# A windowed attention and MLP kernel: head-halves order in the first batch, additive masks through TensorE, strided reads when transposed tiles leave PSUM, full-depth sink values, score units in pairs

## The chip, the core and the metric

The kernel runs on one NeuronCore of a Trainium2 chip. TensorE (PE) multiplies matrices into PSUM, VectorE (DVE) and ScalarE (ACT) read PSUM and work on SBUF, GpSimd (POOL) works on SBUF alone, and SyncE (SP) issues every DMA from one queue, in program order. Each engine runs its own instructions in order; semaphores tie the engines together. The metric is device microseconds for one launch.

## The reference

Four batches, eight heads, 768 positions, head size 64. Attention with 4 sink positions and a window of 128, then a residual MLP over the 512 features, with a product over tokens in front:

```python
scores = q @ k.T / 8                       # per head, 768 x 768
keep = (col < 4) | ((row - col >= 0) & (row - col < 128))
a = softmax(where(keep, scores, -1e9))
x = (a @ v) as [batch, 768, 512]
a1 = alpha1 * x + beta1
u  = x + lam * einsum('ts,bsd->btd', w_tok, a1)
a2 = alpha2 * u + beta2
out = u + lam * (relu(a2 @ w_ch1) @ w_ch2) # 512 -> 2048 -> 512
```

All inputs and outputs are float32 in DRAM; the kernel works in fp16 with fp32 sums.

## The kernel before

**Tiles.** The sequence is six tiles of 128 rows. Heads come in four pairs (`hp`), and G is a half of the heads (four of them, two pairs). A window of 128 means that key tile j meets query tiles j and j+1 only, so a score unit (j, G) is 128 keys by 256 queries by four heads.

**Attention of a batch.** `load_qk` brings q or k of a head pair (eight DMAs of 384 KB, six buffers), `cast_qk` makes it fp16, and `trans` does six TensorE transposes into one PSUM tile `tp` and copies that to `qkT` on VectorE (L175). Partition p of a loaded tile holds six neighbouring positions, so the copy has to interleave: before, it reads PSUM in order and writes every sixth fp16 element of SBUF. `sinks` multiplies all queries from 256 on with the four sink keys and takes the exponential (`es`). `scores` does four matmuls (L200, each on 64 rows of the array), one exponential over 128x1024 (L207) into `E`, and `mask` multiplies `E` with a 0/1 mask on VectorE (L218). `pv` multiplies `es` with the sink values `vs` (L227, 64 rows) and two `E` tiles with `vf`, which has a column of ones for the sum of the softmax; `norm` divides (L250, L251) and, with both halves there, makes `xh` on GpSimd (L257, L258). `vs` is filled by eight small DMAs out of `vf`.

**Dense part of a batch.** `dense` gives a list of slots: six `tok` (six matmuls of 512 columns, an add L310, an fp16 cast L312), `uT` (transposes of that, L325, and a scale and shift on VectorE, L330), 32 `mlp1` (four matmuls of 384 columns, L345, and a Relu on ScalarE, L350), and 24 `mlp2` (four of 512 columns, L362; after four slots an add, L368, and the store). Transposes, `tok`, `uT`, `mlp1`, `mlp2` and the sinks share three PSUM buffers (tag "d").

**What sets the order.** The schedule is written out by hand. The first batch's attention is in line, mixed with loading and casting the weights; then a loop over batches walks the slots of `dense(b)` and after slot i runs `side[i]`: the next batch's casts, transposes, sinks, score units and `pv`, spread evenly over the slots, and for b = 0 the casting and loading of the MLP weights. Weights pass through two staging buffers (tag "wst"), so a weight's DMA waits on SP for the cast of the weight two before it, and everything behind it on SP waits too.

Of the kernel before, what the change touches and what calls it, by code (L numbers as in the profile page):

```python
# [14 lines left out]
def kernel(  # L15
# [20 lines left out]
    P = 128  # L36
# [12 lines left out]
    assert window == P and 0 < n_sink <= 16, (n_sink, window)  # L49
# [11 lines left out]
    def load_qk(b, hp, t):  # L61
        nat = sb.tile([P, 2, NR * D], FP32, tag="nat", bufs=6, name=f"nat{b}_{hp}_{t}")
# [43 lines left out]
    )  # L106

# [38 lines left out]
    def cast_qk(b, hp, t, eng):  # L146
        nat = nat_tiles.pop((b, hp, t))
        d = sb.tile([P, NR, P], FP16, tag="n16", bufs=4, name=f"n16_{b}_{hp}_{t}")
        o = d.rearrange("p r (e d) -> p e r d", e=2)
        i = nat.rearrange("p e (r d) -> p e r d", r=NR)  # L150
# [27 lines left out]
    def sinks(b):  # L178
        for e in range(2):
            nc.vector.tensor_copy(  # L180
                ks[64 * e : 64 * e + 64, :, e * n_sink : (e + 1) * n_sink],
                qkT[b].rearrange("p (a t) s -> p a t s", t=2)[64 * e : 64 * e + 64, :, 1, 0:n_sink],
            )
        pt = ps.tile([P, S - 2 * P], FP32, tag="d", bufs=3, name=f"sk{b}")
        for hp in range(HP):
# [58 lines left out]
    def norm(b, r, G):  # L244
        po = pv_ps.pop((b, r, G))
        if G == 0:
            x_t[b, r] = sb.tile([P, H, D], FP32, tag="x", bufs=12, name=f"x{b}_{r}")
        x = x_t[b, r]
# [4 lines left out]
        if G == 1:  # L253
# [325 lines left out]
```

## Time and profile before

| | |
|---|---|
| median of 3 runs | 383.55 us (382.33 to 385.0) |
| profiled execution: time, span | 382.78 us, 381.1 us |
| PE, DVE, ACT, POOL busy | 286.6, 206.8, 132.5, 120.9 us |
| first score matmul starts | 31.24 us |
| `tok` of batch 0, 1, 2, 3 starts | 70.90, 165.85, 245.30, 326.13 us |
| first `mlp1` of batch 0, first `mlp2` of batch 0 | 80.23, 135.97 us |
| mean granted TensorE clock | 0.928 of full speed |

The span runs from the first to the last instruction. Since the matmuls of `tok` open each batch's dense part, their starts cut the span into periods: 0 to 165.85 us holds the first batch's attention and dense part with the second batch's attention, then come two alike periods, and from 326.13 us the last dense part alone. The sum of busy times says little by itself, because these stretches have different limits.

### The profile page before, as it was taken

Reading aid. Unit: us, or ns where it says so; the run is one execution under the profiler, and the core shown is the slowest. Engines: PE = TensorE matmul, PEld = TensorE weight load, DVE = VectorE, ACT = ScalarE, POOL = GpSimd, SP = SyncE. Lnnn points to the kernel's source line nnn. Section 1 sums busy time; section 2 is a strip of 40 time slices with the busy share of each in tenths; the row PEclk is TensorE's granted clock in tenths of the full one; section 3 lists DMA queues with packets and bytes.
Section 4 is the critical chain, followed back from the end, with each engine's and each line's share of the span. In section 5 each row is a group of like instructions: output and inputs, shape, how many; then the busy total and the mean of one; then the engine's idle time right before and its main releaser. Section 6 shows DMA issues by size and latency. Waiting matters only on the chain.

```text
span 381.1 us, 4896 instructions
## 1 busy us (share of the span) xinstructions
PE 286.6 (75%) x1956; PEld 144.9 (38%) x1956; DVE 206.8 (54%) x289; ACT 132.5 (35%) x208; POOL 120.9 (32%) x121
## 2 busy tenths in 40 slices
PE   1313655899336699996649999984489999999996
PEld 1211422355113244443425544443245444455542
DVE  6894576255299566539983434279924443440021
ACT  1004536186101363212229731022258520267300
POOL 3200298308276035674001452723004425000000
PEclk9999965699955699999899999999989999999999
DMA  7912662339960009542000039340000011100012
GB/s 248 328 30 83 140 221 98 124 105 344 264 212 15 2 22 306 141 140 55 0 2 0 3 120 269 138 138 0 0 2 0 3 55 57 55 3 0 10 74 83
DMA packets 43927, 37.03 MB, mean 97 GB/s; under 512 B 27393, under 2 KB 35585, under 8 KB 43905
## 3 DMA queue, kind: packets, MB, share of 16 engines
q1 hardware_dynamic: 43904, 36.73, 31.2%
q8 instruction: 15, 0.25, 0.3%
q14 instruction: 8, 0.06, 0.0%
HBM read 30.41 MB, written 6.29 MB: 96 GB/s over the span
## 4 chain that ended last, share of the span: by engine, by line
PE 56%; DVE 26%; DMA 5%; ACT 3%; SPq 3%; issue 3%; POOL 3%; DVEq 0%; ACTq 0%
PE ch L362 22%; DVE qkT L175 19%; PE h L345 16%; PE tok L305 7%; PE S L200 3%; PE pv L235 2%; DMA wst_w<-in_moe_w_ch_dram 2%; PE pv L227 2%; DMA vnat<-in_v_dram 2%; PE tp L174 1%; PE pv L239 1%; ACT w1f L429 1%; SPq L166 1%; DMA la_b<-in_moe_alpha_dram 1%; DVE w2f L435 1%
## 5 line engine op out<-in xcount | busy, mean ns | idle before, releaser
L345 PE MATMUL h<-uT,w1f 128*128 128x384 f16 x512 | 101.0, 344 | 12.8 <-DVE qkT L175 11.8
L362 PE MATMUL ch<-w2f,hT 128*128 128x512 f16 x384 | 89.9, 379 | 0.0
L175 DVE COPY qkT<-tp 128x768 f16<-128x768 f16 x32 | 84.5, 2774 | 7.7 <-PE tp L174 7.6
L350 ACT ACTIVATE hT<-h 128x384 f16<-128x384 f32 x128 | 61.9, 492 | 74.3 <-PE h L345 73.6
L345 PEld LDWEIGHTS <-w1f 128*128 128x128 f16 x512 | 48.7, 101 | 49.1 <-issue 24.9
L257 POOL TENSOR_TENSOR tmp<-x,la_b 128x512 f32<-128x512 f32 x24 | 30.9, 1287 | 109.6 <-DVE x L251 109.6
L207 ACT ACTIVATE E<-S 128x1024 f16<-128x1024 f32 x40 | 40.9, 1022 | 36.4 <-PE S L200 36.3
L174 PE MATMUL tp<-iden,n 128*128 128x128 f16 x192 | 19.5, 256 | 42.4 <-DVE n L154 18.9
L368 DVE TENSOR_TENSOR x<-x,ch 128x512 f32<-128x512 f32 x24 | 16.5, 688 | 63.9 <-PE ch L362 63.9
L362 PEld LDWEIGHTS <-hT 128*128 128x128 f16 x384 | 34.7, 98 | 38.8 <-issue 2.7
L218 DVE TENSOR_TENSOR E<-E,maskn 128x1024 f16<-128x1024 f16 x32 | 27.4, 857 | 26.9 <-ACT E L207 26.8
L312 ACT CAST u<-x 128x512 f16<-128x512 f32 x24 | 14.8, 617 | 71.3 <-DVE x L310 69.0
L305 PE MATMUL tok<-xh,wtokT 128*128 128x512 f16 x144 | 35.3, 401 | 2.2 <-POOL xh L258 1.3
L258 POOL TENSOR_TENSOR xh<-tmp,lb_b 128x512 f16<-128x512 f32 x24 | 34.5, 1437 | 1.9
L174 PEld LDWEIGHTS <-n 128*128 128x128 f16 x192 | 15.8, 116 | 50.0 <-DVE n L154 19.7
L154 POOL CAST n<-nat 128x768 f16<-128x768 f32 x28 | 23.5, 845 | 32.4 <-issue 24.1
L310 DVE TENSOR_TENSOR x<-x,tok 128x512 f32<-128x512 f32 x24 | 16.5, 687 | 16.7 <-PE tok L305 16.6
L305 PEld LDWEIGHTS <-wtokT 128*128 128x128 f16 x144 | 14.5, 102 | 20.9 <-issue 5.7
L251 DVE TENSOR_TENSOR x<-pv,rec 128x256 f32<-128x256 f32 x48 | 20.4, 424 | 1.8 <-DVE rec L250 0.2
L435 POOL TENSOR_TENSOR w2f<-wst_w,lam_b 128x512 f16<-128x512 f32 x8 | 13.5, 1704 | 20.5 <-DMA wst_w<-in_moe_w_ch_dram 20.5
L162 POOL CAST vf<-vnat 128x512 f16<-128x512 f32 x24 | 16.2, 675 | 10.7 <-DMA vnat<-in_v_dram 6.9
L235 PE MATMUL pv<-vf,E 128*128 128x65 f16 x160 | 17.1, 205 | 2.3 <-DVE x L251 2.3
(47 smaller groups left out, 183.0 us busy)
## 6 DMA issues: line engine op xcount, KB each, us to landing
wst_w<-in_moe_w_ch_dram SPq DMA_DIRECT2D x8, 1024.0 KB
nat<-in_q_dram SPq DMA_DIRECT2D x16, 384.0 KB
nat<-in_k_dram SPq DMA_DIRECT2D x16, 384.0 KB
vnat<-in_v_dram SPq DMA_DIRECT2D x24, 256.0 KB
out_dram<-x SPq DMA_DIRECT2D x24, 256.0 KB
wst_t<-in_moe_w_tok_dram SPq DMA_DIRECT2D x3, 768.0 KB
vs<-vf SPq DMA_DIRECT2D x32, 0.5 KB
lam_b<-in_moe_lam_dram SPq DMA_DIRECT2D x1, 256.0 KB
```

What stands on the lines that cost most here:

```text
L154: eng.tensor_copy(o, i)
L174: nc.tensor.transpose(pt[:, r, :], src[:, r, :], iden)
L175: nc.vector.tensor_copy(qkT[b][:, 2 * hp + t, :].rearrange("p (i r) -> p r i", r=NR), pt)
L207: nc.scalar.activation(eT, pS, AF.Exp, scale=scale)
L218: nc.vector.tensor_mul(ev, ev, m.to_broadcast(list(ev.shape)))
L235: nc.tensor.matmul(po[:, hl, :], E[b, r - 1, G][:, e, i, P : 2 * P], vf[r - 1][:, h, :], start=(r == 1), stop=False,)
L257: nc.gpsimd.tensor_mul(tmp, xf, la1_b)
L258: nc.gpsimd.tensor_add(xh, tmp, lb1_b)
L305: nc.tensor.matmul(pt, wtokT[:, si, ti * P : (ti + 1) * P], xh_t[b, si], start=(si == 0), stop=(si == NR - 1),)
L345: nc.tensor.matmul(ph, w1f[:, c, fi * P : (fi + 1) * P], uT[0][:, c, chk * NTOK : (chk + 1) * NTOK], start=(c == 0), stop=(c == NC - 1),)
L350: nc.scalar.activation(hT[chk][:, fi, :], ph, AF.Relu)
L362: nc.tensor.matmul(pch[ti], hT[chk][:, fi, nt * P : (nt + 1) * P], w2f[:, fi, :], start=(fi == 0), stop=(fi == NF - 1),)
```

## The change

1. **Strided read.** `trans` writes the transposes to PSUM as before; the copy to `qkT` now reads PSUM with a step of 128 fp16 elements (256 bytes) and writes SBUF in order. In the first batch two of the eight copies are on ScalarE.
2. **First batch by head halves.** Two head pairs are loaded, cast and transposed; their six score and six `pv` steps run while the other two pairs are cast and transposed; then the other half follows. Masks are not multiplied: two matmuls per unit with the identity put -30000 or 0 into PSUM, and the score matmuls add to it. `xh` leaves out beta1, which comes back in `residual` as the row sum of `w_tok` times lam times beta1.
3. **Loads.** All of the first batch, the sink values, the constants, `w_tok` and the first quarter of `w_ch1` are issued at the start into buffers that stand idle then. The later weight loads stay behind the two staging buffers. The prefetch has eight q/k tiles in place of six.
4. **Casts of weights.** `w_tok` is cast in six pieces: three in the second half of the attention, three between the `tok` slots of batch 0. Each quarter of `w_ch1` is cast half on ScalarE, half on GpSimd. Batch 0 walks `mlp1` by quarters of `w_ch1`.
5. **Later batches.** The sink product is 128 rows deep (`vs` is zero where a head has no business) and `vs` is filled by one GpSimd multiply from a DMA of its own. Two score units stand back to back. Every third Relu is on VectorE.

```diff
-        pt = ps.tile([P, NR, P], FP16, tag="d", bufs=3, name=f"tp{b}_{hp}_{t}")
+        pt = ps.tile([P, S], FP16, tag="d", bufs=3, name=f"tp{b}_{hp}_{t}")
+        o = qkT[b][:, 2 * hp + t, :]
         for r in range(NR):
-            nc.tensor.transpose(pt[:, r, :], src[:, r, :], iden)
-        nc.vector.tensor_copy(
-            qkT[b][:, 2 * hp + t, :].rearrange("p (i r) -> p r i", r=NR), pt)
+            nc.tensor.transpose(pt[:, r * P : (r + 1) * P], src[:, r, :], iden)
+        copy(eng or nc.vector, o.rearrange("p (i r) -> p i r", r=NR),
+             pt.rearrange("p (r i) -> p i r", r=NR))
...
+        if bias:
+            bt = bias0 if j == 0 else (biasn if j < NR - 1 else biasn[:, :, 0:P])
+            for e in range(2):
+                nc.tensor.matmul(pS[:, e], iden, bt.to_broadcast([P, n, w]), start=True, stop=False)
...
-            g = slice(64 * G, 64 * G + 64)
+            g = slice(64 * G, 64 * G + 64) if b == 0 else slice(0, P)
...
+    def fill_vs(b):
+        nc.gpsimd.tensor_mul(vs[b % 2][:, :, 0:D], vsn.pop(b), bmf.to_broadcast([P, H, D]))
...
-        def mk_s(i):
+        def mk_s(j):
             def f():
-                sc[i] = scores(b, *S_ORDER[i])
+                if j < NR - 1:
+                    for G in range(2):
+                        sc[j, G] = scores(b, j, G)
...
-                nc.scalar.activation(hT[chk][:, fi, :], ph, AF.Relu)
+                if fi % 3 == 2:
+                    nc.vector.tensor_scalar_max(hT[chk][:, fi, :], ph, 0.0)
+                else:
+                    nc.scalar.activation(hT[chk][:, fi, :], ph, AF.Relu)
...
+    def cast_wtok(ti, eng):
+        w = sb.tile([P, NR, P], FP16, tag="n16", bufs=4, name=f"wt16_{ti}")
+        wf = w.rearrange("p r i -> p (r i)")
+        nc.scalar.activation(wf, wtn[ti // 3][:, ti % 3, :], AF.Copy, accum_out=rs[:, ti : ti + 1])
+        pt = ps.tile([P, NR, P], FP16, tag="d", bufs=3, name=f"wT{ti}")
+        for si in range(NR):
+            nc.tensor.transpose(pt[:, si, :], w[:, si, :], iden)
+        copy(eng, wtokT[:, :, ti * P : (ti + 1) * P], pt)
...
+    for (hp, t), ce, ee in zip(QK_ORDER[:4], (V, A, G_, V), (V, A, V, A)):
+        cast_qk(0, hp, t, ce)
+        trans(0, hp, t, ee)
...
+    scores(0, 0, 0, True)
+    scores(0, 1, 0, True)
+    sinks(0, (0,))
...
+    scores(0, 4, 1, True)
+    cast_wtok(1, V)
+    cast_v0(1, 5, G_)
+    pvn0(3, 1)
+    scores(0, 5, 1, True)
+    cast_wtok(2, V)
+    pvn0(4, 1)
+    pvn0(5, 1)
     load_w1(1)
...
+    tok[0]()
+    cast_wtok(3, V)
+    tok[1]()
+    cast_wtok(4, V)
+    tok[2]()
+    cast_wtok(5, V)
+    for f in uT0:
+        f()
+    tok[3]()
+    tok[4]()
+    tok[5]()
+    cast_w1(1, (A, G_))
     load_w1(3)
...
-            side[6].append(lambda: (cast_w1(2), load_w2(0)))
-            side[10].append(lambda: (cast_w1(3), load_w2(1)))
-            side[20].append(lambda: (cast_w2(0), load_w2(2)))
-            side[24].append(lambda: (cast_w2(1), load_w2(3)))
-            side[28].append(lambda: cast_w2(2))
-            side[32].append(lambda: cast_w2(3))
+            side[5].append(lambda: (cast_w1(2, (A, G_)), load_w2(0)))
+            side[12].append(lambda: (cast_w1(3, (A, G_)), load_w2(1)))
+            side[19].append(lambda: (cast_w2(0, (V, G_, V, G_)), load_w2(2)))
+            side[23].append(lambda: (cast_w2(1, (V, G_, V, G_)), load_w2(3)))
+            side[27].append(lambda: cast_w2(2, (V, G_, V, G_)))
+            side[31].append(lambda: cast_w2(3, (V, G_, V, G_)))
...
             if b == 0:
-                side[11].append(lambda nb=nb: prefetch(nb))
+                side[6].append(lambda nb=nb: prefetch(nb))
```

**Order on ScalarE where the dense part of batch 0 begins.** `wt16` is a sixth of `w_tok` in fp16, `u16` the cast after a `tok`, `w1f` the cast of a quarter of `w_ch1`. Before:

```order
L429 CAST w1f_118<-wst_w1_0_308 128x4x512
L207 ACTIVATE E0_5_None_529<-S0_5_None_520 128x1024
L429 CAST w1f_118<-wst_w1_1_350 128x4x512
L312 CAST u16_0_0_591<-x0_0_301 128x512
L312 CAST u16_0_1_601<-x0_1_370 128x512
L312 CAST u16_0_2_611<-x0_2_417 128x512
```

The same place in the changed kernel:

```order
L472 ACTIVATE wt16_2_543,rs_71<-wtn0_109 128x768
L208 CAST w1f_165<-wst_w1_0_113 128x2x512
L391 CAST u16_0_0_597<-x0_0_244 128x512
L472 ACTIVATE wt16_3_599,rs_71<-wtn1_115 128x768
L391 CAST u16_0_1_618<-x0_1_270 128x512
L472 ACTIVATE wt16_4_620,rs_71<-wtn1_115 128x768
L391 CAST u16_0_2_639<-x0_2_306 128x512
L472 ACTIVATE wt16_5_641,rs_71<-wtn1_115 128x768
```

Three casts of `w_tok` now stand behind the `u16` of the `tok` before them; on PE their transposes stand between the `tok` matmuls, as the diff shows.

**Order of the DMAs on SP around the first prefetch.** `w2` are quarters of `w_ch2`, `nat1` and `vnat1` q, k and v of batch 1. Before:

```order
L387 DMA wst_w2_0_653<-in_moe_w_ch2_dram 128x4x512
L387 DMA wst_w2_1_685<-in_moe_w_ch2_dram 128x4x512
L64 DMA nat1_0_0_693<-in_q_dram 128x2x384
L64 DMA nat1_0_1_695<-in_k_dram 128x2x384
L64 DMA nat1_1_0_697<-in_q_dram 128x2x384
```

Now:

```order
L69 DMA vnat1_2_793<-in_v_dram 128x8x64
L69 DMA vnat1_3_795<-in_v_dram 128x8x64
L77 DMA vsn1_797<-in_v_dram 32x8x64 x4
L110 DMA wst_w2_1_840<-in_moe_w_ch2_dram 128x4x512
L110 DMA wst_w2_2_888<-in_moe_w_ch2_dram 128x4x512
L110 DMA wst_w2_3_943<-in_moe_w_ch2_dram 128x4x512
```

Before, two quarters of `w_ch2` went ahead of the prefetch and two behind it; now one goes ahead (row not shown) and three follow the whole prefetch.

**Order on VectorE behind the second quarter of `w_ch2`**, in the changed kernel:

```order
L487 TENSOR_TENSOR w2f_166<-wst_w2_1_840,lam_b_66 128x512 x2
L210 COPY qkT1_908<-tp1_1_0_947 128x768
L210 COPY qkT1_908<-tp1_1_1_966 128x768
L210 COPY qkT1_908<-tp1_2_0_985 128x768
L430 TENSOR_SCALAR hT0_0_707<-h0_0_14_994 128x384
L210 COPY qkT1_908<-tp1_2_1_1002 128x768
L487 TENSOR_TENSOR w2f_166<-wst_w2_2_888,lam_b_66 128x512 x2
L210 COPY qkT1_908<-tp1_3_0_1021 128x768
L210 COPY qkT1_908<-tp1_3_1_1036 128x768
```

Six of the eight copies of batch 1 stand behind this multiply. Before, seven stood behind the third quarter's multiply (L435) and three behind the fourth's; now two stand behind the third's and none behind the fourth's.

## Rows read from the trace of the kernel before

**Rows 1.** Chain that ended last, in time: start us, us, what.

```profile
192.86 5.28 DVE qkT L175 x2
...
338.98 17.70 PE h L345 x108
356.68 20.73 PE ch L362 x96
```

**Rows 2.** Busy by stage: stretch, length, PE, PEld, DVE, ACT, POOL, clock, DMA share, GB/s.

```profile
171.10:198.97 27.87, 15.92 (x125) 9.45 (x124) 25.85 (x21) 6.26 (x13) 4.95 (x7) 0.94 0.09 20
198.97:245.30 46.33, 45.82 (x333) 21.65 (x334) 17.82 (x40) 21.35 (x35) 20.51 (x19) 1.00 0.34 103
...
250.55:278.17 27.62, 14.58 (x125) 8.82 (x124) 25.84 (x21) 6.25 (x13) 4.94 (x7) 1.00 0.09 20
278.17:326.13 47.96, 47.45 (x333) 22.17 (x334) 17.82 (x40) 21.54 (x35) 16.11 (x12) 0.96 0.08 29
326.13:381.10 54.97, 51.09 (x285) 26.61 (x282) 12.22 (x21) 19.10 (x38) 0.00 (x0) 1.00 0.09 34
```

**Rows 3.** Groups of instructions by line: busy us, mean ns; idle before.

```profile
L175 DVE COPY qkT<-tp 128x768 f16<-128x768 f16 x32 | 84.5, 2774 | 7.7 <-PE tp L174 7.6
L207 ACT ACTIVATE E<-S 128x1024 f16<-128x1024 f32 x40 | 40.9, 1022 | 36.4 <-PE S L200 36.3
...
L251 DVE TENSOR_TENSOR x<-pv,rec 128x256 f32<-128x256 f32 x48 | 20.4, 424 | 1.8 <-DVE rec L250 0.2
...
L310 DVE TENSOR_TENSOR x<-x,tok 128x512 f32<-128x512 f32 x24 | 16.5, 687 | 16.7 <-PE tok L305 16.6
L312 ACT CAST u<-x 128x512 f16<-128x512 f32 x24 | 14.8, 617 | 71.3 <-DVE x L310 69.0 <-PE uTp L325 2.3
...
L330 DVE TENSOR_SCALAR uT<-uTp,alpha_c,beta_c 128x384 f16<-128x384 f16 x32 | 13.5, 469 | 5.4 <-PE uTp L325 5.3
...
L415 DVE COPY wtokT<-wT 128x768 f16<-128x768 f16 x6 | 3.3, 558 | 8.3 <-PE wT L414 8.1
```

**Rows 4.** Busy time by stage up to batch 1's `tok`, columns as in rows 2.

```profile
0.00:31.24 31.24, 6.58 (x54) 4.82 (x54) 24.88 (x25) 1.28 (x1) 6.60 (x17) 1.00 0.59 185
31.24:70.90 39.66, 21.64 (x189) 11.81 (x186) 20.57 (x41) 19.35 (x17) 22.64 (x18) 0.74 0.50 160
70.90:80.23 9.33, 9.15 (x43) 4.09 (x43) 4.78 (x9) 3.70 (x6) 0.00 (x0) 0.82 0.00 0
80.23:135.97 55.74, 34.45 (x214) 18.37 (x213) 34.93 (x28) 21.15 (x38) 23.51 (x22) 0.79 0.52 161
135.97:165.85 29.88, 29.37 (x226) 12.36 (x223) 16.63 (x36) 8.95 (x10) 18.33 (x15) 1.00 0.55 159
```

**Rows 5.** Timeline of the opening: start, us, engine, line; what ended the idle time.

```profile
9.26 0.83 POOL L154 CAST n<-nat 128x768 f16<-128x768 f32 x1 [3.35 <-DMA nat<-in_k_dram]
...
31.24 0.61 PE L200 MATMUL S<-qkT 64*128 64x256 f16 x4
...
34.32 1.46 PE L414 MATMUL wT<-iden,wt 128*128 128x128 f16 x12 [2.48 <-ACT wt L409]
```

**Rows 6.** Timeline around w2's wait, and DMA over that stretch (as rows 2).

```profile
105.41 2.36 DVE L435 TENSOR_TENSOR w2f<-wst_w,lam_b 128x512 f16<-128x512 f32 x2 [7.41 <-DMA wst_w<-in_moe_w_ch_dram]
...
82.00:109.00 27.00, 14.72 (x105) 8.54 (x102) 12.77 (x12) 11.50 (x22) 13.93 (x12) 0.93 0.98 310
```

**Rows 7.** Timeline of PE around a score unit and a sink product.

```profile
212.95 0.39 PE L200 MATMUL S<-qkT 64*128 64x256 f16 x4
...
213.27 1.47 PE L345 MATMUL h<-uT,w1f 128*128 128x384 f16 x8
...
214.68 0.28 PE L227 MATMUL pv<-vs,es 64*128 64x260 f16 x1
214.89 0.20 PE L235 MATMUL pv<-vf,E 128*128 128x65 f16 x1
...
215.14 0.81 PE L345 MATMUL h<-uT,w1f 128*128 128x384 f16 x4
```

More of the change, by code (lines that the diff above doesn't have):

```diff
@@ L77 @@
+    for r in range(NR):
+        load_v0(1, r)
+    for ti in range(3):
+        load_wtok(ti)
+    load_w1(0)
+    for ti in range(3, NR):
+        load_wtok(ti)
+    nc.sync.dma_start(lb1_b, moe_beta1.unsqueeze(0).to_broadcast([P, DM]))
+    nc.sync.dma_start(alpha2_c, moe_alpha2.rearrange("(c p) -> p c", p=P))
+    nc.sync.dma_start(beta2_c, moe_beta2.rearrange("(c p) -> p c", p=P))
     iden = const.tile([P, P], FP16, name="iden")
@@ L106 @@
     )
+    nc.gpsimd.affine_select(
+        out=bm, in_=bm, compare_op=ALU.is_ge, fill=0.0,
+        base=0, pattern=[[-32, HP], [-n_sink, 2]], channel_multiplier=1,
+    )
+    nc.gpsimd.affine_select(
+        out=bm, in_=bm, compare_op=ALU.is_ge, fill=0.0,
+        base=n_sink - 1, pattern=[[32, HP], [n_sink, 2]], channel_multiplier=-1,
+    )
+    bias0 = const.tile([P, 1, 2 * P], FP16, name="bias0")
+    biasn = const.tile([P, 1, 2 * P], FP16, name="biasn")
+    for m, bb in ((mask0, bias0), (maskn, biasn)):
+        nc.vector.tensor_scalar(
+            out=bb, in0=m, scalar1=-1.0, scalar2=30000.0, op0=ALU.add, op1=ALU.mult)
     vf = []
@@ L144, with copy @@
     xh_t = {}
[L146 to L150, printed above, removed]
+    def copy(eng, o, i):
         if eng is nc.scalar:
@@ L308, in f @@
                     )
+                if b == 0:
+                    residual(b, ti)
                 xf = x_t[b, ti].rearrange("p h d -> p (h d)")
@@ L370, in mk_mlp2 @@
             return f
-        for ti in range(5):
-            slots.append(mk_tok(ti))
-        slots += [mk_uT(0, 0), mk_uT(0, 1), mk_tok(5)]
+        tok = [mk_tok(ti) for ti in range(NR)]
+        mlp2 = [mk_mlp2(ti, part) for ti in range(NR) for part in range(4)]
+        if b == 0:
+            m1 = []
+            for qd in range(4):
+                for chk in range(2):
+                    m1 += [mk_mlp1(chk, fi) for fi in range(4 * qd, 4 * qd + 4)]
+            return tok, [mk_uT(0, 0), mk_uT(0, 1)], [mk_uT(1, 0), mk_uT(1, 1)], m1, mlp2
+        slots += tok[:5] + [mk_uT(0, 0), mk_uT(0, 1)] + tok[5:]
         m1 = [mk_mlp1(0, fi) for fi in range(NF)]
@@ L402 @@
-    sinks(0)
-    core = attn_core(0)
-    wt16 = {}
-    def cast_wtok(w):
-        wt16[w] = sb.tile([P, 2, S], FP16, tag="wt16", bufs=2, name=f"wt16_{w}")
-        nc.scalar.copy(wt16[w], wst.pop(f"t{w}"))
-        for a in range(2):
-            ti = 2 * w + a
-            pt = ps.tile([P, NR, P], FP16, tag="d", bufs=3, name=f"wT{ti}")
-            for si in range(NR):
-                nc.tensor.transpose(pt[:, si, :], wt16[w][:, a, si * P : (si + 1) * P], iden)
-            nc.vector.tensor_copy(wtokT[:, :, ti * P : (ti + 1) * P], pt)
@@ L431, in cast_w2 @@
-    def cast_w2(i):
+        return slots + m1 + [mk_mlp1(1, fi) for fi in range(NF)] + mlp2
+    def cast_wtok(ti, eng):
[6 more added lines that the diff above has]
+        copy(eng, wtokT[:, :, ti * P : (ti + 1) * P], pt)
@@ new lines @@
+    cast_v0(0, 0, G_)
+    cast_v0(0, 1, G_)
+    G_.tensor_mul(la1_b, la1_b, lam_b)
+    scores(0, 0, 0, True)
+    scores(0, 1, 0, True)
+    sinks(0, (0,))
+    cast_v0(0, 2, G_)
+    fill_vs(0)
+    cast_v0(0, 3, G_)
+    pvn0(0, 0)
+    cast_qk(0, 2, 0, G_)
+    scores(0, 2, 0, True)
+    pvn0(1, 0)
+    cast_v0(0, 4, G_)
+    cast_qk(0, 2, 1, G_)
+    trans(0, 2, 0, V)
+    scores(0, 3, 0, True)
+    pvn0(2, 0)
+    cast_v0(0, 5, G_)
+    cast_qk(0, 3, 0, G_)
+    trans(0, 2, 1, V)
+    scores(0, 4, 0, True)
@@ new lines @@
+    pvn0(3, 0)
+    cast_qk(0, 3, 1, G_)
+    trans(0, 3, 0, V)
+    scores(0, 5, 0, True)
+    pvn0(4, 0)
+    cast_v0(1, 0, G_)
+    trans(0, 3, 1, V)
+    scores(0, 0, 1, True)
+    pvn0(5, 0)
+    cast_v0(1, 1, G_)
+    sinks(0, (1,))
+    scores(0, 1, 1, True)
+    cast_v0(1, 2, G_)
+    scores(0, 2, 1, True)
+    pvn0(0, 1)
+    cast_v0(1, 3, G_)
+    pvn0(1, 1)
+    scores(0, 3, 1, True)
+    cast_wtok(0, V)
+    cast_v0(1, 4, G_)
+    pvn0(2, 1)
+    scores(0, 4, 1, True)
+    cast_wtok(1, V)
@@ L475 @@
+    cast_v0(1, 5, G_)
[4 more added lines that the diff above has]
+    pvn0(5, 1)
+    load_w1(1)
+    tok, uT0, uT1, m1, mlp2 = dense(0)
+    G_.tensor_mul(lb1_b, lb1_b, lam_b)
+    cast_w1(0, (A, G_))
+    load_w1(2)
+    tok[0]()
[10 more added lines that the diff above has]
+    cast_w1(1, (A, G_))
     load_w1(3)
+    slots0 = m1 + mlp2
```

293 lines of the change are left out of this document (134 added, 159 removed).

## The prediction

> **What bounds the kernel now.** I read the chain of waits first: over the second half it is TensorE's matmuls, broken by pairs of `qkT` copies of 5.28 us [rows 1]. Then the busy times by stage. Each period of a middle batch has a transposing stage in which VectorE is busy 25.85 of 27.87 us and TensorE 15.92, and a stage of 46 to 48 us in which TensorE is busy throughout [rows 2]; the last dense part, 54.97 us, is TensorE's too. The matmuls are at full speed there: 108 of `mlp1` in 17.70 us (0.164 each), 96 of `mlp2` in 20.73 (0.216) [rows 1]. So a microsecond taken from VectorE counts in the transposing stages and nowhere else in these periods. Before them lie 165.85 us for the first batch, where no engine is full for long: VectorE is busy 24.88 of the first 31.24 us, TensorE 21.64 of the next 39.66, and 34.45 of the 55.74 between the first `mlp1` and the first `mlp2` [rows 4]. There loads and copies set the end, and there the order matters.
>
> **The strided read.** This decides most. The copy takes 2.774 us now, with an SBUF step of six elements; a copy of the same size out of PSUM, in order on both sides, takes 0.558 [rows 3]. These are the two ends, since no row shows a PSUM read with a step like the new one. Between them I take a rate of one element at a time: 256 elements take 0.424 us and 512 take 0.687 on VectorE out of PSUM, so 1.03 ns an element and 0.16 us fixed, which makes 0.95 us for 768 [rows 3]. I choose it because reading apart loses the pairing that the 0.558 shows, and nothing in the rows says that a read far apart costs as the scattered fp16 write does.
>
> The Trainium skill's page "SBUF — State Buffer", section "Door 1: The DMA port swizzle", speaks against this change: an access that leaves a short line pays a penalty, and PSUM's lines are 8 bytes, so all 768 reads would pay. Its page "VectorE: DVE Perf Modes", section "Mode 1× (REGULAR) — the baseline", has odd strides and PSUM operands at one result per cycle and speaks for the middle value. No run here shows either yet; the first rule's time is rival A, the second's the forecast.
>
> **Middle periods.** They last 79.45 and 80.83 us (starts of `tok` in the table). In the transposing stage VectorE loses eight copies of 2.64 and gains eight of 0.95 and four or five Relus of 0.16 + 384 x 1.03 ns = 0.56 us: 25.85 - 21.1 + 7.6 + 2.5 = 14.8. TensorE's 15.92 is then the longer one [rows 2]. They pass tiles to and fro through three PSUM buffers, so neither hides quite under the other: I take 16.5 us, 11 less than now.
>
> In TensorE's own stage a sink product of 64 rows costs more than its columns. Eight `mlp1` matmuls from 213.27 end their issue at 214.58, the product starts at 214.68, and the next matmul, of 260 columns' worth (0.11 us) later, could start at 214.79 but starts at 214.89 [rows 7]. So 0.2 us is lost around each of eight; with 128 rows I take it as gone: 1.6 us. A score unit, also 64 rows deep, takes 0.32 us from 212.95 to 213.27 for two columns of 256 run two abreast, 0.22 [rows 7]; with 0.1 ahead of it, two in a row lose that 0.2 once, over five pairs 1.0 us. The ends are 0 and 2.6; I take 2.6. Relus on VectorE take nothing from the path: TensorE is the limit, and ScalarE is busy only 21 of 46 us [rows 2]. Its two exponentials in a row hold back Relus for 2.04 us [rows 3], about as long as three PSUM buffers of `mlp1` last (3 x 0.66).
> Periods: 5.25 (four `tok`) + 16.5 + 46.33 - 2.6 = 65.5, and 5.25 + 16.5 + 47.96 - 2.6 = 67.1. The last dense part stays at 55.0: its TensorE work is the same.
> Three edits cost nothing as long as their cover holds. The GpSimd multiply that fills `vs` and the sink values' own DMAs, in place of eight small DMAs, lie in stages where GpSimd is busy 21 of 46 us and DMA 0.34 of the time [rows 2]; uncovered, an operation like that is a microsecond or two a batch. `residual` runs on VectorE under the six matmuls of its `tok`; uncovered it is 0.7 us in each of six. The two more prefetched tiles land ahead of need, as the four behind them do now.
>
> **First batch up to its first `tok`.** The fourth q/k tile is there at 9.26 [rows 5]; cast 0.8, six transposes 0.73 (half of 1.46, [rows 5]), copy 0.95: the first scores start at 11.8 instead of 31.24, and need half the heads only. A step of the first half is then two mask matmuls (0.216 each at 2.4 GHz, double at 1.2), four score matmuls (0.39, 0.61 as in the opening), six transposes (0.73 in the opening) and a `pv` (0.46; 214.68 to 215.14) [rows 5, 7]: 1.7 us, or 3.1 at the lower clock. The masks add about 5 us of TensorE at full clock and take 11 multiplies off VectorE. The steps are locked to GpSimd's casts and `xh` halves; I take 2.8 us a step, so the second half starts at 28.8. Of its steps three are a single chain, since TensorE works in order: score, exponential 1.02, `wt16` behind it on ScalarE (768 elements at the rate of [rows 3], 0.617 for 512 to 1.022 for 1024: 0.82), its transposes, `pv`: 3.6 us each at full clock, 4.9 at half. With three units before and two `pv` after, the first `tok` starts between 46.5 and 52; I take 50 (70.90 now). The clock is granted at 0.74 over that stretch now [rows 4], so I lean to the late end.
>
> **From `tok` to `mlp1`.** This gets longer. On ScalarE `wt16` stands behind `u16`, on TensorE the transposes of `wt16` stand ahead of the next `tok`: so three times `tok` 1.3, add 0.69, cast 0.62, `wt16` 0.82, transposes 0.4 and handoffs make 4.1 us at full clock, 5.7 at half, 12 to 17 in all. Then `uT` and three `tok`, 4.6. I take 19 where 9.33 stand now [rows 4]: `mlp1` starts at 69 (80.23 now).
>
> **From `mlp1` to `mlp2`.** The second quarter of `w_ch2` is queued on SP behind the whole prefetch. DMA starts on that after slot 5's cast, 5.8 us in; 6.5 MB (two quarters of 1 MB, eight tiles of 384 KB, v and sink values 1.3 MB) at the 310 GB/s of the like stretch [rows 6] take 21, so the multiply waits on VectorE until 27, as it waited 7.41 us at 105.41 [rows 6]. Behind it stand six copies, and three PSUM buffers soon stop TensorE. After it come about 10 us of copies, transposes and `mlp1`; the fourth quarter, whose buffer comes free at 30.5, is there at 36 and multiplied by 39. I take 40 us where 55.74 stand now: eight copies at 0.95 are the main difference. `mlp2` starts at 109, and its stage of 29.88 loses half of the 2.6: 28.5, so batch 1's `tok` starts at 137.5 (165.85 now).
>
> **Sum.** 137.5 + 65.5 + 67.1 + 55.0 = 325.1 us of span; the profiled execution has 1.7 us around its span, so 327, against its own 382.78. The median of the runs is 0.8 above that execution, which I leave in the rounding.
>
> **Rivals.**
> A. *The read pays as the write did* (2.7 us a copy). For it: the present copy shows that a step can cost 3.4 ns an element. Against it: that step is on fp16 writes to SBUF. Two copies ahead of the first score and one ahead of the second half add 5.5, six behind `w2` 10.6, and the transposing stages return to VectorE with the Relus on top, 14.8 + 8 x 1.76 = 28.9 for 16.5, twice: 327 + 5.5 + 10.6 + 25 = 368.
> B. *The first batch runs tighter.* If the clock is up by 25 us, the chains cost their lower ends: `tok` at 46.5, `mlp1` 17 later, `mlp2` 37 after that, `tok` of batch 1 at 129: 318; with full hiding in the transposing stages 312. For it: more TensorE work per step. Against it: three serial chains.
> C. *The paired exponentials take back what pairs and sinks give.* If each pair stops TensorE 0.7 us in its three buffers, 15 pairs cost 10 us: 338. Against it: a third of the Relus goes to VectorE.
> D. *Slower than before.* Only the same copy could do that: about 25 copies lie on the path (3, 6 and 16), and the margin above A is 15 us, so beyond 2.72 + 0.6 = 3.3 us a copy, 4.1 ns an element, the gain is gone; at twice the present duration it ends near 430. No row shows such a rate on VectorE.
> That the change does not do what it says would be A for its largest part.
>
> **How the numbers follow.** Forecast 0.60, with a range of its own of 314 to 341 (6 us for the first batch's clock, 4 for `w2`, 2 for each period); A 0.13, B 0.13, C 0.10, D 0.02, others near no change 0.02. A read at two cycles an element would add some 20 us and belongs to the forecast's upper tail. The range that leaves out A, D and a little of B: 308 to 349. A change of 1%, about 4 us, is what can be told from none. Faster: all but D and the others, 0.96; same 0.02; slower 0.02.
>
> **What would show it.** In the profile of the changed kernel: the `qkT` copies at 0.9 to 1.0 us on VectorE (step one; 2.7 is A); middle `tok` starts 65 to 68 us apart with VectorE no longer full in the transposing stage; no gap around the sink products; the first score at 12, first `tok` at 46 to 52, first `mlp1` near 69 with ScalarE's `wt16` ending TensorE's waits between the `tok`; a wait of VectorE and GpSimd for `w_ch2` some 27 us after. The prediction is wrong if the copies are slow, or if the periods stay above 72 us with fast copies: then something else than VectorE held the transposing stage.

## The result, and the profile after

| | before | after |
|---|---|---|
| median of 4 runs each, us | 383.94 | 337.41 (335.56 to 342.47) |
| ratio, 95% interval | | 0.8773 (0.873 to 0.8816) |
| profiled execution / its span, us | 382.78 / 381.1 | 335.56 / 333.8 |

Faster, inside the range, 10 us above the predicted 327. The run of 342.47 us, in a slower state, stands in the median and not in the ratio. From the page of the changed kernel, its busy times and its clock in 40 slices:

```profile
PE 275.8 (83%) x1980; PEld 145.0 (43%) x1980; DVE 167.0 (50%) x325; ACT 113.9 (34%) x182; POOL 118.8 (36%) x138
...
PEclk9999567699975999999999999999999999999999
```

The copies of [rows 3] by line (busy, mean ns, idle before):

```profile
L210 DVE COPY qkT<-tp 128x768 f16<-128x768 f16 x30 | 28.4, 953 | 10.5 <-PE tp L234 10.4
...
L210 DVE COPY wtokT<-wT 128x768 f16<-128x768 f16 x6 | 3.3, 558 | 15.6 <-PE wT L475 15.6
L208 ACT COPY qkT<-tp 128x768 f16<-128x768 f16 x2 | 1.6, 800 | 4.9 <-PE tp L234 4.9
```

The strided read costs 953 ns where the strided write cost 2774, and the `wtokT` copy, of the same size and in order on both sides, still 558. Next the stages of the changed kernel, columns as in [rows 2, 4]: opening; 11 to 28 us; 28 to 46 us (the second half of the heads starts at 24.1); `tok` to `mlp1`; `mlp1` to `mlp2`; `mlp2` to batch 1's `tok`; transposing stage; the two parts of a middle period (`tok` to `mlp2`, `mlp2` to `tok`); last dense part. From 146.94 on the cuts lie 0.16 us behind the first matmul, as the starts of `tok` in the table before do; starts named further down are those of the first matmul.

```profile
0.00:11.31 11.31, 3.07 (x24) 2.28 (x25) 4.29 (x18) 2.91 (x3) 4.51 (x17) 1.00 0.86 243
11.31:28.00 16.69, 12.27 (x124) 5.40 (x124) 7.91 (x20) 8.39 (x10) 11.43 (x19) 1.00 0.87 248
28.00:46.00 18.00, 10.94 (x98) 5.28 (x98) 5.32 (x15) 8.09 (x13) 4.96 (x9) 0.67 0.55 188
...
45.08:68.42 23.34, 14.79 (x71) 6.83 (x69) 11.65 (x20) 5.07 (x11) 5.42 (x5) 0.72 0.12 45
...
68.42:114.79 46.37, 29.50 (x202) 17.58 (x201) 23.59 (x33) 15.26 (x28) 22.57 (x23) 0.85 0.74 221
114.79:146.94 32.15, 28.51 (x234) 13.34 (x233) 22.32 (x42) 10.33 (x12) 19.70 (x17) 1.00 0.55 166
...
152.13:168.20 16.07, 14.71 (x129) 9.13 (x127) 13.99 (x24) 5.23 (x11) 7.69 (x11) 1.00 0.15 34
...
146.94:188.92 41.98, 39.32 (x315) 22.28 (x314) 28.00 (x53) 21.81 (x37) 14.09 (x17) 1.00 0.10 31
188.92:212.87 23.95, 23.95 (x167) 11.72 (x166) 9.41 (x23) 2.96 (x3) 13.23 (x12) 1.00 0.62 189
278.81:333.80 54.99, 51.09 (x284) 26.64 (x282) 17.73 (x31) 14.31 (x28) 0.00 (x0) 1.00 0.09 34
```

In the transposing stage, taken to the same point as in [rows 2] (the end of the product with the sink keys), VectorE (third busy time) is no longer full: 13.99 of 16.07 us, where it was 25.85 of 27.87 [rows 2]. The middle periods are 65.9 us. The first batch still has three stretches with TensorE far from full. In the one from 28 to 46 us it waits for each of three casts of `w_tok` (2.00, 2.01 and 1.58 us), the serial chains of the prediction, with the clock at half from about 34 us. Two more waits explain the other two stretches. TensorE between the first `tok`, each time held by a cast of `w_tok` on ScalarE:

```profile
51.84 0.82 PE L475 MATMUL wT<-iden,wt 128*128 128x128 f16 x6 [4.01 <-ACT wt L472]
52.45 2.58 PE L382 MATMUL tok<-xh,wtokT 128*128 128x512 f16 x6
57.30 0.51 PE L475 MATMUL wT<-iden,wt 128*128 128x128 f16 x6 [2.27 <-ACT wt L472]
57.65 2.30 PE L382 MATMUL tok<-xh,wtokT 128*128 128x512 f16 x6
62.22 0.82 PE L475 MATMUL wT<-iden,wt 128*128 128x128 f16 x6 [2.27 <-ACT wt L472]
```

And all engines around the second quarter of `w_ch2`, which answers to [rows 6]:

```profile
99.71 2.36 DVE L487 TENSOR_TENSOR w2f<-wst_w,lam_b 128x512 f16<-128x512 f32 x2 [9.88 <-DMA wst_w<-in_moe_w_ch_dram]
99.76 3.43 POOL L487 TENSOR_TENSOR w2f<-wst_w,lam_b 128x512 f16<-128x512 f32 x2 [11.13 <-DMA wst_w<-in_moe_w_ch_dram]
...
103.14 0.82 POOL L210 CAST n<-nat 128x768 f16<-128x768 f32 x1
...
104.01 0.82 PE L234 MATMUL tp<-iden,n 128*128 128x128 f16 x6 [12.40 <-POOL n L210]
```

VectorE and GpSimd both wait for one transfer; a q/k cast stands behind GpSimd's multiplies, and TensorE waits 12.40 us for that cast, not for a copy of VectorE.

### The profile page after: what moved, and what is told of

It reads as the page before. It is cut to its first block, busy times and chain, and to the rows that moved or that the text cites. A ratio compares the mean times of both kernels' runs of the same rounds, so it can differ in the third digit from the quotient of the medians.

```text
span 333.8 us, 4946 instructions
## 1 busy us (share of the span) xinstructions
PE 275.8 (83%) x1980; PEld 145.0 (43%) x1980; DVE 167.0 (50%) x325; ACT 113.9 (34%) x182; POOL 118.8 (36%) x138
## 4 chain that ended last, share of the span: by engine, by line
PE 56%; DVE 20%; issue 8%; ACT 5%; POOL 5%; SPq 3%; DMA 2%; DVEq 0%; POOLq 0%; ACTq 0%
PE ch L444 22%; PE h L424 15%; PE tok L382 7%; DVE qkT L210 5%; DVE x L389 3%; DVE E L289 3%; PE S L271 3%; DVE uT L409 2%; DVE x L323 2%; POOL n L210 2%; ACT E L278 2%; ACT wt L472 2%; DMA wst_w<-in_moe_w_ch_dram 2%; SPq L96 2%; PE pv L310 1%
## 5 line engine op out<-in xcount | busy, mean ns | idle before, releaser
L424 PE MATMUL h<-uT,w1f 128*128 128x384 f16 x512 | 94.1, 330 | 2.7 <-ACT hT L432 1.4
L432 ACT ACTIVATE hT<-h 128x384 f16<-128x384 f32 x88 | 42.7, 493 | 60.3 <-PE h L424 59.3
L278 ACT ACTIVATE E<-S 128x1024 f16<-128x1024 f32 (+1 forms) x42 | 40.4, 1003 | 29.0 <-PE S L271 29.0
L331 POOL TENSOR_TENSOR tmp<-x,la_b 128x512 f32<-128x512 f32 x18 | 22.8, 1269 | 74.4 <-DVE x L323 74.4
L430 DVE TENSOR_SCALAR hT<-h 128x384 f16<-128x384 f32 x40 | 22.2, 556 | 41.1 <-PE h L424 41.1
L450 DVE TENSOR_TENSOR x<-x,ch 128x512 f32<-128x512 f32 x24 | 16.5, 687 | 46.7 <-PE ch L444 46.7
L210 DVE COPY qkT<-tp 128x768 f16<-128x768 f16 x30 | 28.4, 953 | 10.5 <-PE tp L234 10.4
L210 POOL CAST n<-nat 128x768 f16<-128x768 f32 x29 | 24.4, 859 | 19.0 <-issue 12.9
L234 PEld LDWEIGHTS <-n 128*128 128x128 f16 x192 | 14.2, 107 | 31.4 <-POOL n L210 18.9
L332 POOL TENSOR_TENSOR xh<-tmp,lb_b 128x512 f16<-128x512 f32 x18 | 23.5, 1305 | 1.4
L389 DVE TENSOR_TENSOR x<-x,tok 128x512 f32<-128x512 f32 x24 | 16.5, 688 | 10.8 <-PE tok L382 10.2
L289 DVE TENSOR_TENSOR E<-E,maskn 128x1024 f16<-128x1024 f16 x24 | 18.5, 772 | 1.4 <-ACT E L278 1.4
L487 POOL TENSOR_TENSOR w2f<-wst_w,lam_b 128x512 f16<-128x512 f32 x8 | 11.8, 1496 | 15.4 <-DMA wst_w<-in_moe_w_ch_dram 15.4
```

The lines of the kernel that those rows point to most:

```text
L234: nc.tensor.transpose(pt[:, r * P : (r + 1) * P], src[:, r, :], iden)
L289: nc.vector.tensor_mul(ev, ev, m.to_broadcast(list(ev.shape)))
L331: nc.gpsimd.tensor_mul(tmp, xf, la1_b)
L332: nc.gpsimd.tensor_add(xh_t[b, r], tmp, lb1_b)
L389: nc.vector.tensor_add(xf, xf, pt)
L424: nc.tensor.matmul(ph, w1f[:, c, fi * P : (fi + 1) * P], uT[0][:, c, chk * NTOK : (chk + 1) * NTOK], start=(c == 0), stop=(c == NC - 1),)
```

## The experiments

Times are medians; ratios are to the kernel before on the same chip (381.9 to 383.9 us there), with 95% intervals. Where the interval of a kernel overlaps that of the changed one, the ratios do not part the two, and the reading rests on the stages. Points in time are those of each profiled execution.

**The strided read alone, in the kernel before.**
```diff
-            qkT[b][:, 2 * hp + t, :].rearrange("p (i r) -> p r i", r=NR), pt)
+            qkT[b][:, 2 * hp + t, :].rearrange("p (i r) -> p i r", r=NR),
+            pt.rearrange("p r i -> p i r"))
```


> The kernel before, with the strided read alone: the copy of each q/k tile reads PSUM with a step and writes SBUF in order; nothing else is changed. Theory (the copy is most of the gain): the copy falls from 2.77 to 0.95 us, each of the two transposing stages loses 11 us, the opening 10 to 15 (eight copies on its path, less where the loads then bound it), the stretch from mlp1 to mlp2 about 10 (eight copies). That makes 336 to 350 us, and I take 343; what is left to the changed kernel's 337.4 is the worth of all other edits together, 0 to 12 us. Rival (the copy only pays together with the new order and the Relus on VectorE): two thirds of the gain stay away and it ends above 360.


Measured 337.68 us, 0.8834 (0.8779 to 0.889): not told apart from the whole change. Its stages (`S` to `tok`, `tok` to `mlp1`, `mlp1` to `mlp2`, `mlp2` to `tok`):

```profile
19.56:54.49 34.93, 19.76 (x184) 11.29 (x181) 20.06 (x39) 19.34 (x17) 20.74 (x17) 1.00 0.54 159
54.49:67.45 12.96, 11.50 (x53) 4.86 (x50) 5.39 (x11) 3.71 (x6) 2.71 (x3) 1.00 0.19 70
67.45:116.55 49.10, 33.07 (x214) 17.94 (x213) 20.54 (x28) 21.12 (x38) 22.84 (x22) 0.79 0.60 183
116.55:146.27 29.72, 29.21 (x225) 12.26 (x222) 16.62 (x36) 8.95 (x10) 18.17 (x15) 1.00 0.54 160
```

The new order's `tok` starts 9.4 us earlier (45.08 against 54.49), and its way from there to `mlp1` is 10.4 longer: at the first `mlp1` nothing is left (68.42 against 67.45). Batch 1's `tok` starts at 146.8 and 146.3. Only the middle periods, 65.9 us against 67.1, are shorter with the rest of the change.

**The old write, in the changed kernel.**
```diff
-        copy(eng or nc.vector, o.rearrange("p (i r) -> p i r", r=NR),
-             pt.rearrange("p (r i) -> p i r", r=NR))
+        copy(eng or nc.vector, o.rearrange("p (i r) -> p r i", r=NR),
+             pt.rearrange("p (r i) -> p r i", r=NR))
```


> The changed kernel with the old copy: PSUM read in order, SBUF written with the step. Theory (rival A's sum, carried over to the measured time): transposing stages back to VectorE, about 12 us more in each of two, three copies in the first half of the first batch, 5 to 6, six behind the second quarter of w_ch2, about 10: 337.4 + 40 = 378, range 365 to 385. VectorE's copies at 2.7 us; what ScalarE's two cost with scattered writes no run shows yet. Rival (other things bound the first batch, GpSimd's casts and loads, so the copies there are hidden): only the transposing stages lose, 337.4 + 25 = 362.


Measured 383.6 us, 1.0017 (0.9971 to 1.0063): all of the gain is gone. By line:

```profile
L210 DVE COPY qkT<-tp 128x768 f16<-128x768 f16 x30 | 80.9, 2734 | 4.6 <-PE tp L234 4.5
...
L208 ACT COPY qkT<-tp 128x768 f16<-128x768 f16 x2 | 5.4, 2714 | 4.5 <-PE tp L234 4.5
```

ScalarE pays for the scattered write as VectorE does. Against the changed kernel each middle period is 12.6 us longer (78.5), `mlp1` to `mlp2` 10.5 (56.9): rival A's terms of 12.5 and 10.6. The way to the first `tok` is 12.4 longer (57.44), where 5.5 were reckoned; why was not taken apart.

**The prefetch earlier.** Deleted at slot 6 of `mlp1`, and:
```diff
     load_w1(2)
+    prefetch(1)
     tok[0]()
```


> The changed kernel with the prefetch of batch 1 issued behind the third load of w_ch1, some 50 us into the kernel, and no longer between the first and second quarter of w_ch2. Theory (the second quarter behind the prefetch is what makes the stretch from the first mlp1 to the first mlp2 46.4 us long): the waits of VectorE (9.88 us) and GpSimd (11.13 us) for it go, GpSimd's q/k casts are no longer late, and mlp2 follows mlp1 after 38 to 41 us: 329 to 332 us in all. Rival 1 (the load is not what ends it; the half clock or VectorE's copies are): 336 to 338. Rival 2 (4.4 MB of prefetch now stand ahead of the fourth load of w_ch1, and that becomes late): a wait of GpSimd or ScalarE for w_ch1 in the first mlp1, 338 to 345.


Measured 327.73 us, 0.8576 (0.8528 to 0.8624). Its `mlp1` to `mlp2`:

```profile
69.11:106.88 37.77, 29.37 (x201) 16.81 (x200) 24.64 (x35) 15.78 (x29) 24.11 (x24) 0.92 0.47 154
```

37.8 us for 46.4, a little better than the 38 to 41 of the theory; both rivals fall. GpSimd does wait 20.9 us for `w_ch1` there, and nobody waits for it. The move frees the transfer and GpSimd's queue together, so it does not part the two.

**The `w_tok` casts ahead of the first `tok`.**
```diff
+    for ti in range(3, NR):
+        cast_wt16(ti)
     cast_w1(0, (A, G_))
```
(`cast_wtok` then only transposes and copies those three.)


> The changed kernel with the three late casts of w_tok (wt16 3 to 5) issued on ScalarE ahead of the first tok, and so no longer behind the u16 of each tok. Theory: TensorE's three waits for them (4.01, 2.27 and 2.27 us) go, and with them the chain tok, add, u16, wt16, transposes; the first mlp1 starts at 60 to 63 us instead of 68.4. What of that reaches the end: all of it, 330 to 332, if the loads of w_ch1 and w_ch2 move up with ScalarE's casts that free their buffers; rival: less than 2 us of it, 336 to 338, if the second quarter of w_ch2 still sets when mlp2 starts.


Measured 330.01 us, 0.8638 (0.8583 to 0.8693). The first `tok` starts at 46.55 and `mlp1` at 61.16, 14.6 us later where 23.3 stood; of the 7.3 us gained at `mlp1`, 4.9 reach batch 1's `tok` (141.87), since `mlp1` to `mlp2` grows to 48.7. The time is the theory's; by what arrives at that `tok` it lies between theory and rival, nearer the theory.

**The norm ahead of the mask.**
```diff
-                if (j, G) in sc:
-                    mask(sc[j, G], j)
                 if j > 0:
                     pv(b, j - 1, G)
                     norm(b, j - 1, G)
+                if (j, G) in sc:
+                    mask(sc[j, G], j)
```


> The changed kernel with the norm ahead of the mask in VectorE's order, in each step of the next batch's attention. Theory: the stage from the first mlp2 of batch 0 to the tok of batch 1 (32.0 us where 28.5 were forecast) is long because the one PSUM buffer of pv waits for a norm that stands behind a mask; it falls to 29 or 30, the middle periods by up to 1 us each: 333 to 336. Rival (it is the pairs of score units that hold TensorE there, not the norm's place): 337 to 338, the stage at 32.


Measured 332.71 us, 0.8703 (0.8633 to 0.8773). `mlp2` to `tok` falls from 32.0 to 29.5 (115.26 to 144.81), and the middle periods to 64.65, a little more than expected. TensorE's two longest waits of that stage in the changed kernel, each for a norm:

```profile
133.65 0.28 PE L298 MATMUL pv<-vs,es 128*128 128x260 f16 x1 [1.36 <-DVE x L323]
...
138.71 0.28 PE L298 MATMUL pv<-vs,es 128*128 128x260 f16 x1 [1.15 <-DVE x L323]
```

All its waits for norms there add up to 3.5 us, and to 1.2 with the norm first.

**Score units one by one.** `mk_s(j)` issues one unit, and the steps are score, `pv`, score, `pv`.


> The changed kernel with score units issued one by one, as before. Theory of the forecast: a pair saves 0.2 us, five pairs 1.0 a batch, so singles cost 1 us in each middle period: 339 to 340. Rival C in one stage: in the stage before batch 1's tok the pair is what makes 32.0 us of 29.7 (which the kernel before with the strided read alone takes there); then that stage falls to about 30, and with periods up to 1 us longer the time is 335 to 338.


Measured 339.69 us, 0.8883 (0.8807 to 0.8959). Its profiled execution lost 7.7 us before `mlp2`, with the clock down and the `ks` copies late, so the total says little of pairs. The two parts of its middle period do:

```profile
153.10:194.45 41.35, 38.78 (x306) 21.58 (x304) 28.20 (x52) 21.00 (x36) 16.00 (x19) 1.00 0.14 42
194.45:219.00 24.55, 24.55 (x178) 11.92 (x177) 10.35 (x23) 4.26 (x5) 13.56 (x12) 1.00 0.67 192
```

Against 41.98 and 23.95 of the changed kernel: in the part where TensorE is full (the second row) pairs save 0.6 us, in the part with `mlp1` they cost as much, and the period is the same, 65.90. The stage before batch 1's `tok` falls only from 32.0 to 30.6, so pairs are at most 1.4 us of the 3.65 by which it was missed.

**Sink products over 64 rows.**
```diff
-            g = slice(64 * G, 64 * G + 64) if b == 0 else slice(0, P)
+            g = slice(64 * G, 64 * G + 64)
```


> The changed kernel with sink products over 64 rows in all batches, as before. Theory of the forecast: 0.2 us lost around each of eight products a batch, so 1.6 us more in each middle period and up to 1.6 in the stage before batch 1's tok: 340 to 342. Rival: all edits but the copy together make a middle period 1.1 us shorter (65.9 against 67.1 with the strided read alone), so the sinks are worth less than 1 us a period: 337 to 340.


Measured 340.18 us, 0.8895 (0.8828 to 0.8963). The periods are 67.26, so eight products cost 1.33 us, 0.17 each. The theory's 0.2 was nearly right; the rival, which read the sinks' worth from the difference of all edits together, was not: other edits take some of it back (the Relus below).

**All Relus on ScalarE.** The branch on `fi % 3` is taken out.


> The changed kernel with all Relus on ScalarE, as before. Theory of the forecast (TensorE is the limit in the middle periods; two exponentials hold the Relus back 2.04 us, about as long as three PSUM buffers last): 0 to 1 us longer in each middle period, 337 to 340. Rival C's mechanism (each pair stops TensorE some 0.7 us when no Relu is on VectorE): 3 us or more in each middle period, 343 or above.


Measured 332.78 us, 0.8704 (0.8665 to 0.8743): against both expectations. Its middle period, in the same two parts:

```profile
147.71:188.11 40.40, 38.96 (x316) 22.42 (x314) 24.22 (x43) 25.84 (x47) 14.24 (x17) 1.00 0.10 29
188.11:212.06 23.95, 23.95 (x172) 11.72 (x169) 9.56 (x23) 2.96 (x3) 13.23 (x12) 1.00 0.65 192
```

1.58 us less, all of it in the part with `mlp1`, with TensorE nearly as busy (38.96 and 39.32). So the Relus on VectorE do hold TensorE up there: 0.45 us of it before the next batch's product with the sink keys (`sk`), 1.13 after it. TensorE at that product and at the last `pv` of the part, in the changed kernel and then with all Relus on ScalarE:

```profile
167.81 0.40 PE L249 MATMUL sk<-qkT,ks 128*32 128x512 f16 x4 [0.47 <-DVE ks L243]
...
188.39 0.28 PE L298 MATMUL pv<-vs,es 128*128 128x260 f16 x1 [0.80 <-DVE x L323]
```
```profile
168.29 0.40 PE L249 MATMUL sk<-qkT,ks 128*32 128x512 f16 x4
...
187.75 0.28 PE L298 MATMUL pv<-vs,es 128*128 128x260 f16 x1 [0.27 <-DVE x L323]
```

In the changed kernel a Relu of 0.56 us stands on VectorE right ahead of the copies to `ks` (at 166.96) and of the mask and norm (at 186.63). These two waits make 1.0 of the 1.58 us; the rest was not taken apart.

**Masks by multiplication in the first batch.** No mask matmuls; `mask(eT, j)` on VectorE right behind each exponential.


> The changed kernel with the first batch's masks by multiplication on VectorE behind the exponential, in place of the two mask matmuls ahead of each score. Theory of the forecast (steps are locked to GpSimd's casts and to chains; TensorE's five us of mask matmuls are mostly beside them): the first mlp1 moves by less than 2 us either way, 336 to 339. Rival: TensorE's share is on the path in the first batch, the first mlp1 comes 3 to 5 us earlier, 332 to 335; or the multiply of 0.7 to 0.9 us lengthens each of twelve chains and it comes 4 or more later, above 341.


Measured 344.12 us, 0.8989 (0.8934 to 0.9043). The stretch from the first score to the first `tok`, in the changed kernel and then here:

```profile
11.31:45.08 33.77, 22.29 (x216) 10.31 (x215) 12.62 (x33) 16.49 (x22) 16.40 (x27) 0.84 0.72 223
```
```profile
11.71:52.38 40.67, 21.74 (x192) 11.88 (x191) 22.62 (x45) 16.60 (x22) 16.64 (x27) 1.00 0.57 182
```

A step of it in time (start us, us, engine, what ended the idle time):

```profile
25.66 1.04 DVE L292 TENSOR_TENSOR E<-E,maskn 128x1024 f16<-128x1024 f16 x1 [0.56 <-ACT E L279]
...
26.22 0.82 PE L234 MATMUL tp<-iden,n 128*128 128x128 f16 x6 [0.89 <-POOL n L210]
26.62 0.17 DVE L325 RECIPROCAL rec<-pv 128x4 f32<-128x4 f32 x1
```

40.7 us where the changed kernel takes 33.8, and `mlp1` starts 8.9 later. VectorE waits in order for the exponential (12.0 us over 11 waits up to `mlp1`), then multiplies, and the norm (from 26.62 in the rows) comes only behind that. The rival's second case was right: the additive masks are worth 8 to 9 us in this order. A multiply placed behind the norm was not tried.

**The copy in order on both sides.**
```diff
-        copy(eng or nc.vector, o.rearrange("p (i r) -> p i r", r=NR),
-             pt.rearrange("p (r i) -> p i r", r=NR))
+        copy(eng or nc.vector, o, pt)
```


> The changed kernel with the copy of a q/k tile in order on both sides, 0.56 us by the row of another copy of that size; the reordering of the sequence within a head is left out. Theory (with the copy at 0.95 the transposing stages are TensorE's, and VectorE's 14.5 of 18.9 us no longer set them): middle periods shorter by less than 1 us each, 334 to 338. Rival (TensorE still waits for the copy's return of a PSUM buffer): eight times 0.4 in each period, 3.2 us, and as much in the first batch: 326 to 331.


Measured 334.35 us, 0.8736 (0.8693 to 0.878). Middle periods 64.95, 0.98 less; in the first batch nothing (`mlp1` at 68.78, `mlp2` at 115.19). The step of the read costs 0.4 us a copy (953 ns against 553) and about 1 us of the span (333.8 against 332.6); the ratios do not part the two kernels.

**Three moves together** (prefetch, `w_tok` casts, norm first).


> The changed kernel with three moves together: the prefetch behind the third load of w_ch1, the three late casts of w_tok ahead of the first tok, and in each step of the next batch's attention the norm ahead of the mask on VectorE. Theory (three separate stretches, so the gains add): mlp1 starts at 61 us as with the casts moved, mlp2 38 us later as with the prefetch moved, tok of batch 1 some 30 after that: span 334 - 7 - 8 - 2 = 317, time 319, range 316 to 322. Rival (with mlp1 earlier the loads of w_ch1 and w_ch2 end the stretch again): a wait for w_ch1 or w_ch2 of 3 us or more, 323 to 328.


Measured 317.4 us, 0.8307 (0.8243 to 0.8371): `mlp1` at 60.26, `mlp2` at 100.78, `tok` at 130.79, span 315.3. The gains add, but for 2.7 us in `mlp1` to `mlp2` (40.5 for 37.8), and this is faster than both kernels. The Relus on ScalarE on top of it were not tried.

**The same repairs in the old order**: strided read, prefetch behind `load_w1(2)`, norm first.


> The kernel before with the strided read, the prefetch of batch 1 behind the third load of w_ch1, and the norm ahead of the mask; the first batch keeps its old order (all heads at once, masks by multiplication). It tells what the new order of the first batch is worth when both orders are freed of the late loads. Theory (the new order gains up to tok and gives it back only through its chain of w_tok casts and the loads, so freed of both it is ahead): the first mlp1 at 67 us as with the strided read alone, mlp2 some 42 after it (49.1 with the late loads), then 29 to tok, periods of 65.8, end 55: span 325, time 326, against 317.4 for the changed kernel with its three moves. Rival (the two orders are worth the same): 317 to 320.


Measured 329.34 us, 0.8606 (0.856 to 0.8652). `mlp1` at 66.02, `mlp2` at 107.27, `tok` at 136.74, periods 66.8. The theory said 326. Against the three moves together the new order does lead, by 5.8 us at `mlp1` and 6.0 at batch 1's `tok`, once its chain and its loads are mended; as it was made, it led by nothing there.

## Why the prediction was right, and where it missed

**The strided read** was the step that decided, as said, and its rate was right: 0.95 forecast, 0.953 measured. The Trainium skill's page "VectorE: DVE Perf Modes", section "Mode 1× (REGULAR) — the baseline", has one result per cycle there, and the trace agrees as far as it can: 768 results in 953 ns are the rate of the fp32 reads in [rows 3]. The Trainium skill's page "SBUF — State Buffer", section "Door 1: The DMA port swizzle", has a penalty for leaving a short line and, for PSUM, speaks of matmuls; beyond that rate none shows in these reads, neither on VectorE (953 ns) nor on ScalarE (800). What the prediction did not see is how much it decided: alone it gives 0.8834, and without it the rest gives 1.0017. The new order of the first batch, which filled most of the prediction, was worth nothing net up to batch 1's `tok`.

**Middle periods:** 65.5 and 67.1 forecast, 65.9 and 65.9 measured. The transposing stage is right, 16.1 us for 16.5; the parts of the rest were less right than the sum. The sink gap: 1.6 forecast, 1.33 measured. Pairs: 1.0 forecast, 0.6 gained in one part and lost in the other. "Relus on VectorE take nothing from the path" is the step that failed: they take 1.6 us a period. TensorE being the limit of a stage on average did not make the other engines' queues free in it: VectorE, with a Relu ahead of the `ks` copies and of a norm, answered some 0.5 us later twice, and TensorE stood.

**Up to `mlp1`:** 69 forecast, 68.4 measured, and that is luck, out of two errors that nearly cancel. `tok` started at 45.1 and not 50, since the second half started at 24.1 and not 28.8: a step of the first half took 2.1 us and not 2.8. The mask matmuls that open the two halves:

```profile
11.31 1.06 PE L267 MATMUL S<-bias,iden 128*128 128x512 f16 x2
...
24.14 0.59 PE L267 MATMUL S<-bias,iden 128*128 128x512 f16 x2
```

And the way to `mlp1` took 23.3 and not 19: its three rounds took 17.1 us (45.08 to 62.22), the upper end of the forecast, where 14.4 were taken, and the rest 6.2 where 4.6 were. The 9.33 us that the prediction sets beside the 19 are too few. The table's 70.90 is the sixth matmul of the first `tok`, behind a wait; in the kernel before the first one starts at 67.30, 12.9 us ahead of `mlp1`:

```profile
67.30 2.32 PE L305 MATMUL tok<-xh,wtokT 128*128 128x512 f16 x5
70.90 1.44 PE L305 MATMUL tok<-xh,wtokT 128*128 128x512 f16 x3 [1.28 <-POOL xh L258]
```

The mechanism, `wt16` behind `u16` on ScalarE, is shown by the waits and by the cast moved. The adds had one more wait than reckoned: the residual of the first `tok` stood 2.1 us for `lb1_b`, whose multiply on GpSimd stands behind the last `xh` half. What the masks through TensorE save was not priced at all; against the multiplies of the experiment it is 7 us before `tok`.

**`mlp1` to `mlp2`:** 40 forecast, 46.4 measured: the largest miss, 6.4 of the span's 8.7. The wait was foreseen and is the cause (37.8 without it); its size was not. The first of the transfers was issued at 76.54, 8.1 us in and not 5.8, and they took 23.2 us and not 21, so the second quarter was there at 99.71, 31.3 in and not 27. Behind it stood not only VectorE's copies but GpSimd's q/k casts, 3.43 us late, and the clock was at half after TensorE's 12.40 us of standing still: four `mlp1` matmuls at 104.63 took 1.49 us, 0.81 at full clock.

**`mlp2` to `tok`:** 28.5 forecast, 32.15 measured, the other large miss, 3.65. Missed: one PSUM buffer of `pv` whose norm stands behind a mask of the pair on VectorE. With the norm first it is 29.5, and one such wait of 1.2 us is left.

**The rivals.** A, and D with it, is refuted by the 953 ns; with the old write put back the time is 383.6 us, where A's sum gave 368; 10 of the difference are the forecast's own miss. B came in part: `tok` started even before its 46.5, although the clock was at half from about 34 to 48 us; its 17 and 37 us behind that did not come (23.3 and 46.4). C gave 338, within a microsecond of the result, for the wrong reason: with single units the periods are the same, and with all Relus on ScalarE, where C expects a loss, the pairs cost nothing.

## What to carry to other kernels

When a bulk copy between PSUM and SBUF must reorder, put the step on the PSUM read and write SBUF in order, and try that alone before anything is rearranged around it. A reordered schedule can lose behind one queue all that it gained before: after moving work, list for each in-order queue what now stands behind a load or a long chain, and mend that in the same change. Work moved onto an engine that TensorE waits for has a price, even where that engine is half idle on average.

## What the runs showed of the hardware that was not expected

The same fp16 copy of 128 x 768 with a step of six elements in SBUF takes 2734 ns on VectorE and 2714 on ScalarE; with the step on the PSUM side 953 and 800.

After like work the granted clock can differ. Between 37 and 41 us the changed kernel's TensorE was at 1.2 GHz (0.50), the one with multiplied masks at 2.4 (1.00), with fewer matmuls in hand (columns as in [rows 2]; at half speed the same work shows a longer busy time, as the 1.49 us for 0.81 above). The changed kernel's rows, then the other's:

```profile
33.00:37.00 4.00, 2.50 (x21) 0.97 (x21) 1.17 (x3) 1.34 (x4) 1.07 (x2) 0.65 0.36 85
37.00:41.00 4.00, 2.46 (x21) 1.36 (x21) 1.17 (x3) 1.39 (x4) 0.68 (x1) 0.50 0.80 262
```
```profile
33.00:37.00 4.00, 1.91 (x14) 0.79 (x14) 1.39 (x5) 2.52 (x3) 1.44 (x3) 1.00 0.05 8
37.00:41.00 4.00, 1.16 (x12) 0.60 (x12) 2.22 (x6) 1.47 (x3) 2.14 (x4) 1.00 0.00 0
```

In the 9 us before these rows, all at 1.00, TensorE had been busy 5.2 us in the first and 5.7 in the second. Why only one of them lost its clock stays open.
